# Whole rows of the last expert weights, two engines in source order, and copies out of two PSUM banks in a chunked-attention, MoE and soft-MoE kernel

## Chip, cores, metric

One core of one Trainium2 chip. The metric is device time in microseconds (us) of one launch, median over runs. Engines: TensorE (PE), VectorE (DVE), ScalarE (ACT), GpSimd (POOL), SyncE (SP, which here only issues DMAs).

## What is computed

Three layers in a row, all in float32 at the interface:

```python
out  = softmax(scale * q_c @ k_c.T) @ v_c          # chunks of 64 in a sequence of 576, 8 batches, 8 heads
x    = square(relu(x @ w_in)) @ w_out              # 4608 x 512, inner width 2048
logits = x @ phi                                   # 4608 x 32 (8 experts, 4 slots each)
d    = softmax over the 4608 tokens;  slot_input = d.T @ x          # 32 x 512
h_e  = relu(slot_input_e @ w1[e]);  slot_out_e = h_e @ w2[e]        # w1: 8 x 512 x 1024, w2: 8 x 1024 x 512
out  = softmax over the 32 slots (logits) @ slot_out                # 4608 x 512
```

The expert weights w1 and w2 are 16.78 MB each, the output is 9.44 MB.

## The kernel before

36 token tiles of 128 tokens (two batches of 64 tokens each) go through attention and the first MoE layer in blocks of three, a long pipeline that ends when the last block's logits are there. The change lies behind that point, in three stages.

**The chain.** `soft(b)` (lines 849 to 952) takes a block's logits, scales them (`Ls`, L854), spreads them by a matmul (L864), takes the largest (L874 to L876), forms `dts` by an exponential (L877), turns it (L917), and adds `dd` times the tiles `G` to the running sum `acc` (24 records of L928, then L939). For the last block, `slot_turn` (L803) transposes `acc` into one PSUM bank, `slot_rows_of` (L811) multiplies by w_out (`wo`) into another, `slot_inputs` (L824) makes `siT`. Both copies out of PSUM go through `halves` (L799): ScalarE takes the left half of the bank, VectorE the right. Beside the chain, `c_two` prepares four of nine groups of transposed token weights `cT`: a PE transpose (L1047), two ScalarE copies each (L1055, L1060), a subtraction on POOL (L1061) and POOL copies (L197) for the next two groups.

**The experts.** 32 units of w1 and 32 of w2, 512 KB each, are loaded by SP in the order of `units`, each into two free half buffers of 128 x 512 floats. A unit goes as one DMA if the two halves lie side by side (L985 for w1, L994 for w2), else as two (L988, L999). Buffers come free by `give` and `release`: the last four `G` tiles, which hold six units, once L928 has read them, the `wo` buffers once `slot_rows_of` has, and then each weight after its matmul. A unit of w2 is a column half: 4 x 128 rows by 256 columns, so each piece is 1 KB. All of column half 0 is multiplied first (L1584 into `sop`), then all of half 1.

**The output.** Once a column half is summed, `slot_rows` and `slot_parts` form `s4_h[ch]` (ScalarE L1492, PE L1497, ScalarE L1499, VectorE L1501), and `out_group` multiplies it by `cT` (L1553), copies to `o` (L1555 VectorE, L1557 ScalarE) and stores 128 x 4 x 256 pieces (L1568). The four tiles that straddle batches ("lone") go as eight DMAs of 64 KB per column half (L1574).

**Order.** In the tail PE runs in source order by hand (`ST_ORDER`). ScalarE, VectorE, POOL and SP run in the order that a scheduler with a timeline model of its own chose when the program was built.

Of the kernel before, what the change touches and what calls it, by code (L numbers as in the profile page):

```python
# [20 lines left out]
P = 128  # L21
CH = 64
# [52 lines left out]
def kernel(  # L75
# [723 lines left out]
    def halves(out, in_):  # L799
        n = in_.shape[-1] // 2  # L800
        act.activation(out=out[:, :n], in_=in_[:, :n], func=ACTF.Copy)
        dve.tensor_copy(out[:, n:], in_[:, n:])

    def slot_turn():
        ps = misc()
        for c in range(QF):
            pe.transpose(ps[:, c * P : (c + 1) * P], acc[:, c * P : (c + 1) * P], ident)
        fin["yz"] = yz = big.tile([P, 2, DM], F32, tag="g1", name="yz")
        yT = yz[:, 0]
        halves(yT, ps)  # L810

    def slot_rows_of():
        ps = misc()
        yT = fin["yz"][:, 0].rearrange("p (c g s) -> p c g s", c=QF, s=NS)
        for c in range(QF):
            for g in range(NQ):
                pe.matmul(
                    ps[NS * g : NS * g + NS], yT[:, c, g], wo[QF * g + c],
                    start=(c == 0), stop=(c == QF - 1), tile_position=(0, NS * g),
                    skip_group_check=True,  # L820
                )
        halves(fin["yz"][:, 1], ps)
# [26 lines left out]
    def soft(b):  # L849
        s0, n = blocks[NB if b == 1 else b]  # L850
        last = s0 + n == NT
        L, iv = L_ps.pop(b), iv2_all[:, s0 : s0 + n]
# [105 lines left out]
    RT = 1024 // DH  # L958
    units = [(0, 0, 4 * g + e, kk) for g in range(2) for kk in range(KT) for e in range(4)]
# [10 lines left out]
    def load_units():  # L970
        while todo and len(free) > 1:

            whole = [x for x in range(len(free) - 1) if free[x][0] is free[x + 1][0]]
            x = whole[0] if whole else 0
            a, b = free[x : x + 2]
            del free[x : x + 2]
            u = todo.pop(0)
            m, ch, e, kk = u
            whole_home = a[0] is b[0] and a[1] + 512 == b[1]
            places = [t[:, o : o + 512] for t, o, _ in (a, b)]  # L980
            home[u] = (a, b)
            if m == 0:
                src = w1[e, kk * P : (kk + 1) * P, :]
                if whole_home:
                    sp.dma_start(out=a[0][:, a[1] : a[1] + 1024], in_=src)  # L985
                else:
                    for h, pl in enumerate(places):
                        sp.dma_start(out=pl, in_=src[:, h * 512 : (h + 1) * 512])  # L988
            else:
                src = w2[e, kk * RT * P : (kk + 1) * RT * P, ch * DH : (ch + 1) * DH].rearrange(  # L990
                    "(t p) d -> p t d", p=P
                )
                if whole_home:
                    sp.dma_start(  # L994
                        out=a[0][:, a[1] : a[1] + 1024].rearrange("p (t d) -> p t d", d=DH), in_=src
                    )
                else:
                    for h, pl in enumerate(places):
                        sp.dma_start(  # L999
                            out=pl.rearrange("p (t d) -> p t d", d=DH), in_=src[:, h * RT // 2 : (h + 1) * RT // 2]  # L1000
                        )
# [443 lines left out]
    def hidden_T(g, hs):  # L1445
        hT_g[g] = take([P, FT, P], F32, "hT")
        for h in range(2):
            htp = ps2.tile([P, FT // 2, P], F32, tag=f"ht{h}", name="htp")
            for ft in range(FT // 2):
                f0 = (h * FT // 2 + ft) * P  # L1450
                pe.transpose(htp[:, ft], hs[:, f0 : f0 + P], ident)
# [10 lines left out]
    for g in range(2):  # L1462
        hps_g[g] = [ps2.tile([P, 512], F32, tag=f"eh{g}{h}", name="ehps") for h in range(2)]
        for kk in range(KT):
            for hf in range(2):
                for ei in range(4):
# [3 lines left out]
                        part_of((0, 0, e, kk), hf),  # L1470
# [3 lines left out]
                for ei in range(4):  # L1474
                    release((0, 0, 4 * g + ei, kk), hf)
# [32 lines left out]
    GT = 1536 // DH  # L1508
    out_groups, lone = [], []
    for bp in range(NT // CPB):  # L1510
        i0 = bp * CPB
        pairs = [i for i in range(i0, i0 + CPB) if i % 2 == 0 and in_pairs(i)]
        lone += [(i, None) for i in range(i0, i0 + CPB) if not in_pairs(i)]
        for c in range(2):
            group_ = [(i, c) for i in pairs]
            if not out_groups:

                out_groups.append(group_[:2])
                group_ = group_[2:]
            out_groups.append(group_)  # L1520
        if len(lone) == 4:
            out_groups.append(lone)
            lone = []
    assert not lone

    def out_buffer():

        if not todo:
            tags = [t for _, _, t in free]
            for tag in tags:  # L1530
                if size_of[tag] == 1024 and tags.count(tag) == 2:
                    free[:] = [x for x in free if x[2] != tag]
                    return big.tile([P, 4, DH], F32, tag=tag, name="o")
        group_no[0] += 1
        return big.tile([P, GT, DH], F32, tag=out_tags[group_no[0] % 3], name="o")

    step = 512 // DH
    BANKS = sum(-(-len(x) // step) for x in out_groups)
    banks = ("eh00", "eh01", "eh10", "eh11", "ht0")
    bank, group_no = [0], [0]  # L1540

    def out_group(ch, x):

        parts = out_groups[x]
        n = len(parts)
        o = out_buffer()
        for j0 in range(0, n, step):
            m = min(step, n - j0)
            ops = ps2.tile([P, step, DH], F32, tag=banks[bank[0] % 5], name="ops")
            for j in range(m):  # L1550
                i, c = parts[j0 + j]
                rows = cT[i // 8][:, i % 8 + (c or 0)]
                pe.matmul(ops[:, j], rows, s4_h[ch], start=True, stop=True)  # L1553
            if bank[0] % 2:
                dve.tensor_copy(o[:, j0 : j0 + m], ops[:, :m])  # L1555
            else:
                act.activation(out=o[:, j0 : j0 + m], in_=ops[:, :m], func=ACTF.Copy)  # L1557
            bank[0] += 1
            yield

        def at_(i, c):
            bp, ci = divmod(i, CPB)
            return (2 * bp + c) * S + ci * CH

        cols = slice(ch * DH, (ch + 1) * DH)
        if parts[0][1] is not None:
            r0 = at_(*parts[0])
            sp.dma_start(  # L1568
                out=out[r0 : r0 + n * P, cols].rearrange("(t p) d -> p t d", p=P), in_=o[:, :n]
            )  # L1570
        else:
            for j, c in ((j, c) for j in range(n) for c in range(2)):
                r0 = at_(parts[j][0], c)
                sp.dma_start(out=out[r0 : r0 + CH, cols], in_=o[CH * c : CH * c + CH, j])  # L1574

    pending, outs = None, []
    for ch in range(NCH):
        sop = ps2.tile([P, DH], F32, tag=f"so{ch % 2}", name="sop")
        for x in range(2 * FT):
            g, ft = divmod(x, FT)  # L1580
            kk, t = divmod(ft, RT)
            for ei in range(4):
                u = (1, ch, 4 * g + ei, kk)
                pe.matmul(  # L1584
                    sop[32 * ei : 32 * ei + 32], hT_g[g][:, ft, 32 * ei : 32 * ei + 32],
                    part_of(u, t // (RT // 2))[:, t % (RT // 2) * DH : (t % (RT // 2) + 1) * DH],
                    start=(x == 0), stop=(x == 2 * FT - 1),
                    tile_position=(0, 32 * ei), skip_group_check=True,
                )
            if (t + 1) % (RT // 2) == 0:  # L1590
                for ei in range(4):
                    release((1, ch, 4 * g + ei, kk), t // (RT // 2))
                load_units()
            if waiting and x == 1:
                hidden_T(*waiting.pop())
            if pending and x == 0:
                slot_parts(*pending)
                outs = [out_group(ch - 1, y) for y in range(len(out_groups))]
                pending = None
                n_out = 0  # L1600

            if outs and c_todo and x > 1 and x % 2:
                c_group(c_bank("ht1"))
            while outs and n_out < (x - 2) * BANKS // (2 * FT - 3):
                n_out += 1
                while outs and next(outs[0], StopIteration) is StopIteration:
                    outs.pop(0)
        pending = (ch, slot_rows(ch, sop))
        while outs:
            while outs and next(outs[0], StopIteration) is StopIteration:  # L1610
                outs.pop(0)
    slot_parts(*pending)
    for y in range(len(out_groups)):
        for _ in out_group(NCH - 1, y):
            pass
# [30 lines left out]
```

## Time and profile before

| | us |
|---|---|
| median of 3 runs | 772.77 (772.29 to 775.29) |
| profiled execution, its own time | 774.87 |
| profiled execution, span | 773.1 |
| PE busy | 711.1 (92%) |
| DMA queue of SP, time of its packets | 57.7% of 16 engines' span |

PE is busy for 92% of the span, but that is an average over stages. The page's 40 slices of 19.3 us each tell the stages apart: in the last four the DMA engines are full and PE is not.

### The profile page before, as it was taken

What the parts mean: (1) busy time and instruction counts of PE and PEld (TensorE: products, weight loads), DVE (VectorE), ACT (ScalarE), POOL (GpSimd) and SP (SyncE); (2) the same over time, 40 slices, a digit from 0 to 9 for tenths busy, and PEclk for the clock granted to TensorE, in tenths of its full rate; (3) what the DMA queues carried; (4) which work ended last, traced back from release to release, by engine and by line L of the source; (5) the groups of instructions that cost most, each with busy time, mean ns of one, the idle gap of its engine ahead of it and who ended that gap; (6) DMA issues with size and microseconds to landing.
All of it is one profiled execution on the core that took longest, in us unless ns stands there. A gap on an engine that the chain in (4) does not pass through costs nothing.

```text
span 773.1 us, 16704 instructions
## 1 busy us (share of the span) xinstructions
PE 711.1 (92%) x6612; PEld 457.7 (59%) x6612; DVE 428.1 (55%) x908; ACT 457.3 (59%) x951; POOL 161.9 (21%) x209
## 2 busy tenths in 40 slices
PE   5788999898999999999999999999999999969790
PEld 3677776665666566565665656666666565524350
DVE  4789996267756656567665566566656201012160
ACT  3668787664656666666676566566766555531150
POOL 3222221131222312223132231322223100030000
PEclk9799999999999999999999999999999999999995
DMA  7897933233455534455544655454556523759998
GB/s 158 215 257 180 218 123 124 72 66 83 98 117 103 103 76 97 91 103 104 101 97 83 103 101 112 75 103 89 99 88 171 159 69 112 277 178 354 347 355 255
DMA packets 242589, 110.47 MB, mean 143 GB/s; under 512 B 201808, under 2 KB 235600, under 8 KB 242512
## 3 DMA queue, kind: packets, MB, share of 16 engines
q1 hardware_dynamic: 242512, 109.41, 57.7%
q8 instruction: 52, 0.85, 0.5%
q14 instruction: 25, 0.20, 0.1%
HBM read 78.71 MB, written 9.44 MB: 114 GB/s over the span
## 4 chain that ended last, share of the span: by engine, by line
PE 71%; DMA 10%; DVE 9%; ACT 4%; issue 1%; POOL 1%; SPq 1%; DVEq 0%; POOLq 0%; ACTq 0%
PE hps L727 41%; PE gT L761 7%; PE misc L928 4%; PE L L778 4%; DMA unit<-in_moe_w_dram 3%; PE ehps L1468 2%; DVE qk L276 2%; DMA qkT<-qk 2%; DMA qkv<-in_k_dram 2%; DMA qkv<-in_q_dram 1%; PE misc L332 1%; DMA qkv<-in_v_dram 1%; DVE stage L281 1%; PE misc L498 1%; DVE qk L275 1%
## 5 line engine op out<-in xcount | busy, mean ns | idle before, releaser
L727 PE MATMUL hps<-xb,wi 128*128 128x384 f16 (+2 forms) x2400 | 409.2, 321 | 0.3
L727 PEld LDWEIGHTS <-wi 128*128 128x128 f16 x2400 | 225.1, 98 | 139.9 <-issue 18.3
L742 ACT ACTIVATE g<-hps,inv_w 128x384 f32<-128x384 f32 (+1 forms) x200 | 112.6, 563 | 113.0 <-PE hps L727 110.8
L182 DVE TENSOR_REDUCE am<-qkv 128x1 bf16<-128x512 f32 x90 | 61.9, 687 | 89.9 <-DMA qkv<-in_v_dram 45.8
L188 ACT ACTIVATE G<-gT 128x384 f32<-128x384 f32 (+1 forms) x200 | 94.1, 471 | 17.9 <-PE gT L761 15.3
L761 PE MATMUL gT<-ident,g 128*128 128x128 f32 x576 | 98.3, 278 | 4.6 <-ACT G L188 3.7
L749 ACT ACTIVATE g<-g 128x384 f32<-128x384 f32 (+2 forms) x188 | 96.9, 515 | 1.5
L761 PEld LDWEIGHTS gT<-ident,g 128*128 128x128 f32 x576 | 73.0, 144 | 29.6 <-ACT g L749 7.1
L420 POOL TENSOR_SCALAR vbd<-qkv,as 64x512 f16<-64x512 f32 x54 | 37.2, 689 | 87.5 <-PE misc L500 71.8
L471 POOL TENSOR_TENSOR ex<-ex,rs 128x512 f32<-128x512 f32 x27 | 29.3, 1083 | 122.4 <-DVE rs L468 110.3
L410 DVE SCALAR_TENSOR_TENSOR qk<-qkv,as,qk 128x512 f16<-128x512 f32 x54 | 39.7, 762 | 20.4 <-ACT qk L405 19.8
L425 DVE SCALAR_TENSOR_TENSOR vbd<-qkv,as,vbd 64x512 f16<-64x512 f32 x54 | 44.7, 828 | 0.7
L778 PE MATMUL L<-g,wp 128*32 128x384 f32 x384 | 41.7, 498 | 0.0
L405 ACT ACTIVATE qk<-qkv,as 128x512 f16<-128x512 f32 x54 | 36.8, 717 | 7.9 <-DVE as L215 7.9
L484 POOL TENSOR_TENSOR p<-ex,p 128x512 f16<-128x512 f32 x27 | 36.2, 1341 | 16.5 <-ACT p L481 15.9
L481 ACT ACTIVATE p<-ex 128x512 f16<-128x512 f32 x27 | 17.0, 629 | 34.6 <-POOL ex L471 34.4
L928 PE MATMUL misc<-G,dd 128*32 128x512 f32 x288 | 35.1, 622 | 0.5 <-DVE rs__8963 L936 0.5
L435 DVE COPY qbd<-qkT 64x1024 f16<-64x1024 f16 x54 | 23.3, 431 | 18.3 <-DMA qkT<-qk 17.5
L510 DVE SCALAR_TENSOR_TENSOR xb<-misc,xb 128x512 f16<-128x512 f32 x27 | 18.5, 685 | 26.5 <-ACT xb L504 26.2
L223 POOL TENSOR_SCALAR iv_all<-ai 128x1 f32<-128x1 f32 x27 | 7.4, 273 | 108.5 <-DVE ai L218 107.6
L854 DVE TENSOR_TENSOR Ls<-L,iv_all 128x384 f32<-128x384 f32 x12 | 6.7, 557 | 41.5 <-PE L L778 41.5
L461 ACT ACTIVATE ex<-ex,es 128x512 f32<-128x512 f32 x27 | 19.4, 718 | 17.0 <-DVE ex L455 16.9
(156 smaller groups left out, 1018.9 us busy)
## 6 DMA issues: line engine op xcount, KB each, us to landing
unit<-in_moe_w_dram SPq DMA_DIRECT2D x34, 512.0 KB, 4.5
unit<-in_moe_w_dram SPq DMA_DIRECT2D x60, 256.0 KB, 5.9
qkv<-in_q_dram SPq DMA_DIRECT2D x72, 128.0 KB, 3.3
qkv<-in_k_dram SPq DMA_DIRECT2D x72, 128.0 KB, 3.5
qkv<-in_v_dram SPq DMA_DIRECT2D x72, 128.0 KB, 3.3
stage<-in_moe_w_in_dram SPq DMA_DIRECT2D x16, 512.0 KB, 5.3
stage<-in_moe_w_out_dram SPq DMA_DIRECT2D x16, 512.0 KB, 5.8
out_dram<-o SPq DMA_DIRECT2D x14, 512.0 KB, 6.3
```

The source lines that it names most:

```text
L182: dve.tensor_reduce(out=am, in_=src, axis=AX.X, op=ALU.max, apply_absolute_value=True)
L188: act.activation(out=out, in_=in_, func=ACTF.Copy)
L405: act.activation(out=qk16[:, 2 * a], in_=flat[:, a], func=ACTF.Copy, scale=v["s"][:, a : a + 1])
L410: dve.scalar_tensor_tensor(out=qk16[:, 2 * a + 1], in0=flat[:, a], scalar=v["s"][:, a : a + 1], in1=qk16[:, 2 * a], op0=ALU.mult, op1=ALU. ...
L420: pool.tensor_scalar(out=dst[0], in0=vin, scalar1=v["s"][pr, 2:3], scalar2=1.0, op0=ALU.mult, op1=ALU.mult,)
L425: dve.scalar_tensor_tensor(out=dst[1], in0=vin, scalar=v["s"][pr, 2:3], in1=dst[0], op0=ALU.mult, op1=ALU.subtract,)
L727: pe.matmul(hp, wi[f][:, wl, kt], xb[:, xl, kt], start=(nm == 0), stop=(nm == 3 * KT - 1))
L742: act.activation(out=g, in_=hp, func=ACTF.Relu, scale=sc)
L749: act.activation(out=g, in_=g, func=ACTF.Square)
L761: pe.transpose(gt_ps[b, f][:, j], g[:, j * P : (j + 1) * P], ident)
L778: pe.matmul(L_ps[g0][NS * x : NS * x + NS, :n], wp[:, QF * q + x], g[:, x, :n], start=(q == 0), stop=(q == NQ - 1), tile_position=(0, NS * x),
L928: pe.matmul(y[NS * g : NS * g + NS], dd[:, j], G_q[b, g][:, j], start=(j == 0), stop=(j == n - 1), tile_position=(0, NS * g), skip_group_c ...
```

## The change

1. From the last `soft` on, ScalarE and VectorE also run in source order (`tc.manual_schedule`).
2. `halves` becomes `half_out`: the left and right halves of `acc` transposed, and of the product with `wo`, go into two PSUM banks. ScalarE copies the first bank while PE fills the second, which VectorE copies. The product is 32 matmuls of 256 columns instead of 16 of 512.
3. The units of w2 are whole rows (256 rows x 512 columns, partition p holding rows 2p and 2p+1, 4 KB that lie together) for all of expert group 0 and the first quarter of group 1: 20 units. The last 12 are column halves again, each for four experts. Both column sums are kept at once.
4. The output is stored in another order: column half 0 of batches 0 to 3 while the last weights of half 1 arrive, then whole rows of the lone tiles and of batches 4 to 7, then column half 1 of batches 0 to 3. The five late `cT` groups are made while w2's rows arrive.

```diff
-    def halves(out, in_):
-        n = in_.shape[-1] // 2
-        act.activation(out=out[:, :n], in_=in_[:, :n], func=ACTF.Copy)
-        dve.tensor_copy(out[:, n:], in_[:, n:])
+    def half_out(h, out, in_):
+        copy(("act", "dve")[h], out[:, h * DM // 2 : (h + 1) * DM // 2], in_)
...
+        for h in range(2):
+            ps = misc()[:, : DM // 2]
+            for x in range(QF // 2):
+                c = h * QF // 2 + x
+                pe.transpose(ps[:, x * P : (x + 1) * P], acc[:, c * P : (c + 1) * P], ident)
+            half_out(h, yz[:, 0], ps)
...
         last = s0 + n == NT
+        if last:
+            ctx.enter_context(
+                tc.manual_schedule(engines={mybir.EngineType.Activation, mybir.EngineType.DVE})
+            )
...
+    SPLIT = FT // 4
+    units = [("w1", 4 * g + e, kk) for g in range(2) for kk in range(KT) for e in range(4)]
     units += [
-        (1, ch, 4 * g + e, kk)
-        for ch in range(NCH) for g in range(2) for kk in range(FT // RT) for e in range(4)
+        ("rows", 4 * g + e, m)
+        for g in range(2) for m in range((SPLIT if g else FT) // 2) for e in range(4)
     ]
+    units += [("part", ch, ft) for ch in range(NCH) for ft in range(SPLIT, FT)]
+    def w2_rows(e, m):
+        return w2[e, 2 * P * m : 2 * P * (m + 1)].rearrange("(p t) d -> p t d", t=2)
...
+                src = w2[4:, 2 * P * m : 2 * P * (m + 1), ch * DH : (ch + 1) * DH].rearrange(
+                    "e (p t) d -> p t e d", t=2
+                )[:, ft % 2]
...
+    for ft in range(SPLIT, FT):
+        last_rows(0, ft)
+    slot_parts(0, slot_rows(0, sops[0]))
+    firsts = [quads[0][:2], quads[0][2:], *quads[1:]]
+    for ft in range(SPLIT, FT):
+        if FT - ft < len(firsts):
+            out_group(firsts.pop(0), (0,))
+        last_rows(1, ft)
+    so_sb = slot_rows(1, sops[1])
+    out_group(firsts.pop(0), (0,))
+    slot_parts(1, so_sb)
+    for rows in pairs:
+        out_group(rows, both)
+    for rows in quads:
+        out_group(rows, (1,))
```

ScalarE at the last soft-max, before (`cT` and `c` are the copies beside the chain, `dts` and `al` the exponentials, `yz` the chain's copies):

```order
L188 ACTIVATE G<-gT 128x3x128 x2
L1055 ACTIVATE cT<-cps 128x512
L1060 ACTIVATE c_8518<-cps 64x512
L1055 ACTIVATE cT<-cps 128x512
L1060 ACTIVATE c_8543<-cps 64x512
L877 ACTIVATE dts,rsum<-misc,nm 128x384
L880 ACTIVATE al<-run_m,nm 128x1
L1055 ACTIVATE cT<-cps 128x512
L1060 ACTIVATE c_8946<-cps 64x512
L1055 ACTIVATE cT<-cps 128x512
L1060 ACTIVATE c_8951<-cps 64x512
L801 ACTIVATE yz<-misc 128x256 x2
```

Here four copies beside the chain stand ahead of `dts`, and four ahead of `yz`. The same place in the change:

```order
L188 ACTIVATE G<-gT 128x3x128 x2
L882 ACTIVATE dts,rsum<-misc,nm 128x384
L885 ACTIVATE al<-run_m,nm 128x1
L1063 ACTIVATE cT<-cps 128x512
L1068 ACTIVATE c_8518<-cps 64x512
L1063 ACTIVATE cT<-cps 128x512
L1068 ACTIVATE c_8543<-cps 64x512
L188 ACTIVATE yz<-misc 128x256 x2
L1063 ACTIVATE cT<-cps 128x512
L1068 ACTIVATE c_8948<-cps 64x512
L1063 ACTIVATE cT<-cps 128x512
L1068 ACTIVATE c_8953<-cps 64x512
```

The exponentials move ahead of the first four copies, and the chain's two copies ahead of the second four. POOL's and PE's orders stay the same here, except that PE has 32 narrower matmuls for 16.

SP's last DMAs before, from the last of w1 on:

```order
L985 DMA unit<-in_moe_w_dram 128x1024 x5
L988 DMA unit<-in_moe_w_dram 128x512
L999 DMA unit<-in_moe_w_dram 128x2x256 x3
L994 DMA unit<-in_moe_w_dram 128x4x256 x8
L999 DMA unit<-in_moe_w_dram 128x2x256 x45
L1568 DMA out_dram<-o 128x2x256 x2
L1568 DMA out_dram<-o 128x4x256 x7
L1574 DMA out_dram<-o 64x256 x8
```

After these rows the last three come once more, for column half 1. In the change:

```order
L1004 DMA unit<-in_moe_w_dram 128x1024 x5
L1008 DMA unit<-in_moe_w_dram 128x512 x4
L1004 DMA unit<-in_moe_w_dram 128x1024 x8
L1008 DMA unit<-in_moe_w_dram 128x512 x21
L1008 DMA unit<-in_moe_w_dram 128x2x256 x22
L1004 DMA unit<-in_moe_w_dram 128x4x256
L1555 DMA out_dram<-o 128x2x256 x2
L1555 DMA out_dram<-o 128x4x256 x3
L1555 DMA out_dram<-o 128x2x512
L1563 DMA out_dram<-o 64x2x512 x4
L1555 DMA out_dram<-o 128x2x512 x7
L1555 DMA out_dram<-o 128x4x256 x4
```

The loads of rows have the shapes of w1's loads, and only the last 23 load DMAs have pieces of 1 KB. Of the stores, 16 of 64 KB become four of 256 KB.

## Rows read from the trace of the kernel before

**Rows 1.** The page: DMA busy tenths and GB/s in 40 slices.
```profile
DMA  7897933233455534455544655454556523759998
GB/s 158 215 257 180 218 123 124 72 66 83 98 117 103 103 76 97 91 103 104 101 97 83 103 101 112 75 103 89 99 88 171 159 69 112 277 178 354 347 355 255
```
**Rows 2.** Windows: start:end, length, busy per engine, PE clock, DMA share, GB/s.
```profile
657.00:661.00 4.00, 4.00 (x32) 2.39 (x25) 0.00 (x0) 2.09 (x5) 0.00 (x0) 1.00 1.01 393
677.00:686.00 9.00, 5.71 (x36) 2.06 (x35) 1.96 (x7) 3.07 (x8) 3.68 (x4) 0.81 0.01 4
683.00:684.00 1.00, 1.00 (x8) 0.22 (x4) 0.00 (x0) 0.00 (x0) 0.00 (x0) 0.50 0.00 0
692.00:694.00 2.00, 1.42 (x12) 0.98 (x8) 0.42 (x1) 0.38 (x1) 0.00 (x0) 1.00 0.93 286
696.00:712.00 16.00, 16.00 (x153) 6.17 (x146) 3.44 (x9) 2.12 (x5) 0.00 (x0) 1.00 1.10 356
712.00:740.00 28.00, 22.84 (x243) 11.48 (x242) 6.53 (x10) 6.37 (x12) 2.47 (x4) 1.00 1.09 347
745.00:751.00 6.00, 5.01 (x40) 3.78 (x36) 3.74 (x8) 3.55 (x8) 0.00 (x0) 1.00 1.09 385
752.00:756.00 4.00, 1.66 (x12) 1.33 (x11) 2.66 (x5) 2.06 (x4) 0.00 (x0) 1.00 0.62 187
756.00:768.00 12.00, 0.00 (x0) 0.00 (x0) 0.00 (x0) 0.00 (x0) 0.00 (x0) 0.53 1.03 337
768.00:772.00 4.00, 0.00 (x0) 0.00 (x0) 0.00 (x0) 0.00 (x0) 0.00 (x0) 0.50 0.53 126
```
**Rows 3.** Timeline of the last soft-max: start, us, engine, line, instruction [idle before].
```profile
676.61 0.60 ACT L1055 ACTIVATE cT<-cps 128x512 fp32r<-128x512 f32 x1 [2.32 <-PE cps L1047]
676.96 0.15 DVE L876 TENSOR_SCALAR nm<-rm 128x1 f32<-128x1 f32 x1
677.95 2.48 POOL L1061 TENSOR_TENSOR cT<-c,cT 64x512 fp32r<-64x512 f32 x2 [49.65 <-ACT c L1060]
679.07 0.58 ACT L877 ACTIVATE dts<-misc,nm 128x384 f32<-128x384 f32 x1
680.52 1.20 POOL L197 TENSOR_SCALAR c<-cmat 128x512 f32<-128x512 f32 x2
680.67 4.48 PE L928 MATMUL misc<-G,dd 128*32 128x512 f32 x24 [0.50 <-DVE rs__8963 L936]
685.08 1.09 PE L1047 MATMUL cps<-ident,c 128*128 128x128 f32 x8
```
**Rows 4.** Timeline of an earlier block: the same matmuls.
```profile
605.13 2.78 PE L928 MATMUL misc<-G,dd 128*32 128x512 f32 x24
```
**Rows 5.** Timeline, behind the sum: the chain's copies.
```profile
688.25 0.38 ACT L801 ACTIVATE yz<-misc 128x256 f32<-128x256 f32 x1
688.66 0.42 DVE L802 COPY yz<-misc 128x256 f32<-128x256 f32 x1 [2.62 <-ACT yz L801]
692.47 0.38 ACT L801 ACTIVATE yz<-misc 128x256 f32<-128x256 f32 x1 [3.84 <-PE misc L817]
```
**Rows 6.** Waits of SP's own queue: total us, times, longest.
```profile
SPq L985 <- PE misc L928: 16.8, 2, 12.1
```
**Rows 7.** Timeline of SP: issues of DMAs.
```profile
655.29 0.95 SPq L988 DMA_DIRECT2D unit<-in_moe_w_dram  x2
747.34 6.97 SPq L1574 DMA_DIRECT2D out_dram<-o  x8
763.61 7.11 SPq L1574 DMA_DIRECT2D out_dram<-o  x8
```
**Rows 8.** Timeline, from the last weights' matmuls to the first copies of outputs.
```profile
745.50 0.64 PE L1584 MATMUL sop<-unit,hT 128*32 128x256 f32 x8
749.19 5.47 DVE L1555 COPY o<-ops 128x512 f32<-128x512 f32 x9 [0.83 <-DMA out_dram<-o]
```

More of the change, by code (lines that the diff above doesn't have):

```diff
@@ L797, in prepare_final @@
             dve.memset(second[r : r + 32], -1.0)
-    def halves(out, in_):
-        n = in_.shape[-1] // 2
-        act.activation(out=out[:, :n], in_=in_[:, :n], func=ACTF.Copy)
-        dve.tensor_copy(out[:, n:], in_[:, n:])
+    def half_out(h, out, in_):
+        copy(("act", "dve")[h], out[:, h * DM // 2 : (h + 1) * DM // 2], in_)
     def slot_turn():
-        ps = misc()
-        for c in range(QF):
-            pe.transpose(ps[:, c * P : (c + 1) * P], acc[:, c * P : (c + 1) * P], ident)
         fin["yz"] = yz = big.tile([P, 2, DM], F32, tag="g1", name="yz")
-        yT = yz[:, 0]
-        halves(yT, ps)
+        for h in range(2):
[4 more added lines that the diff above has]
+            half_out(h, yz[:, 0], ps)
     def slot_rows_of():
-        ps = misc()
         yT = fin["yz"][:, 0].rearrange("p (c g s) -> p c g s", c=QF, s=NS)
[L815 to L822, printed above, removed]
+        for h in range(2):
+            ps = misc()[:, : DM // 2]
+            for c in range(QF):
+                for g in range(NQ):
+                    pe.matmul(
+                        ps[NS * g : NS * g + NS], yT[:, c, g],
+                        wo[QF * g + c][:, h * DM // 2 : (h + 1) * DM // 2],
+                        start=(c == 0), stop=(c == QF - 1), tile_position=(0, NS * g),
+                        skip_group_check=True,
+                    )
+            half_out(h, fin["yz"][:, 1], ps)
     def slot_inputs():
@@ L977, in load_units @@
             u = todo.pop(0)
-            m, ch, e, kk = u
             whole_home = a[0] is b[0] and a[1] + 512 == b[1]
-            places = [t[:, o : o + 512] for t, o, _ in (a, b)]
             home[u] = (a, b)
[L982 to L988, printed above, removed]
-            else:
[L990 to L1001, printed above, removed]
+            if u[0] == "w1":
+                _, e, kk = u
+                src = w1[e, kk * P : (kk + 1) * P, :].rearrange("p (h d) -> p h d", h=2)
+            elif u[0] == "rows":
+                src = w2_rows(*u[1:])
+            else:
+                _, ch, ft = u
+                m = ft // 2
+                src = w2[4:, 2 * P * m : 2 * P * (m + 1), ch * DH : (ch + 1) * DH].rearrange(
+                    "e (p t) d -> p t e d", t=2
+                )[:, ft % 2]
+            n = src.shape[1] // 2
+            if whole_home:
+                to = a[0][:, a[1] : a[1] + 1024].rearrange("p (t d) -> p t d", t=2 * n)
+                sp.dma_start(out=to, in_=src)
+            else:
+                for h, (t, o, _) in enumerate((a, b)):
+                    to = t[:, o : o + 512].rearrange("p (t d) -> p t d", t=n)
+                    sp.dma_start(out=to, in_=src[:, h * n : (h + 1) * n])
     def freed(pool_, tag, n):
@@ L1449, in hidden_T @@
             for ft in range(FT // 2):
-                f0 = (h * FT // 2 + ft) * P
-                pe.transpose(htp[:, ft], hs[:, f0 : f0 + P], ident)
+                m, t = divmod(h * FT // 2 + ft, 2)
+                rows = hs[:, 2 * P * m : 2 * P * (m + 1)].rearrange("p (x t) -> p t x", t=2)
+                pe.transpose(htp[:, ft], rows[:, t], ident)
             dst = hT_g[g][:, h * FT // 2 : (h + 1) * FT // 2]
@@ L1504, in slot_parts @@
         s4_h[ch] = s4
[L1508 to L1523, printed above, removed]
@@ L1524 @@
-    assert not lone
-    def out_buffer():
[L1528 to L1538, printed above, removed]
@@ L1539 @@
-    banks = ("eh00", "eh01", "eh10", "eh11", "ht0")
[L1540 to L1551, printed above, removed]
+    def out_buffer():
+        tags = [t for _, _, t in free]
+        for tag in tags:
+            if not todo and 512 * tags.count(tag) == size_of[tag] >= 1024:
+                free[:] = [x for x in free if x[2] != tag]
+                break
+        else:
+            tag = out_ring.pop(0)
+        out_ring.append(tag)
+        return big.tile([P, 1024], F32, tag=tag, name="o")
@@ new lines, with out_group @@
+    out_ring = list(out_tags)
+    banks = ("eh00", "eh01", "eh10", "eh11", "ht0")
+    bank = [0]
+    by_batch = out.rearrange("(b s) d -> s b d", s=S)
+    def out_group(parts, chs):
+        n, w = len(parts), len(chs) * DH
+        flat = out_buffer()
+        items = [(i, c, ch) for i, c in parts for ch in chs]
+        for x0 in range(0, len(items), 2):
+            ops = ps2.tile([P, 2, DH], F32, tag=banks[bank[0] % 5], name="ops")
+            for x, (i, c, ch) in enumerate(items[x0 : x0 + 2]):
@@ L1552, in out_group @@
                 rows = cT[i // 8][:, i % 8 + (c or 0)]
-                pe.matmul(ops[:, j], rows, s4_h[ch], start=True, stop=True)
+                pe.matmul(ops[:, x], rows, s4_h[ch], start=True, stop=True)
+            dst = flat[:, x0 * DH : (x0 + 2) * DH].rearrange("p (x d) -> p x d", x=2)
             if bank[0] % 2:
-                dve.tensor_copy(o[:, j0 : j0 + m], ops[:, :m])
+                dve.tensor_copy(dst, ops)
             else:
-                act.activation(out=o[:, j0 : j0 + m], in_=ops[:, :m], func=ACTF.Copy)
+                act.activation(out=dst, in_=ops, func=ACTF.Copy)
@@ L1558, in out_group @@
             bank[0] += 1
[L1559 to L1565, printed above, removed]
+        o = flat[:, : n * w].rearrange("p (t d) -> p t d", t=n)
+        cols = slice(chs[0] * DH, chs[0] * DH + w)
+        bp, ci = divmod(parts[0][0], CPB)
         if parts[0][1] is not None:
-            r0 = at_(*parts[0])
+            r0 = (2 * bp + parts[0][1]) * S + ci * CH
             sp.dma_start(
-                out=out[r0 : r0 + n * P, cols].rearrange("(t p) d -> p t d", p=P), in_=o[:, :n]
+                out=out[r0 : r0 + n * P, cols].rearrange("(t p) d -> p t d", p=P), in_=o
@@ L1570, in out_group @@
             )
         else:
[L1572 to L1588, printed above, removed]
+            s0, (bq, cj) = ci * CH, divmod(parts[-1][0], CPB)
@@ new lines, in out_group @@
+            assert n == 2 and ci == cj
+            for c in range(2):
+                to = by_batch[s0 : s0 + CH, 2 * bp + c : 2 * bq + c + 1 : 2 * (bq - bp), cols]
+                sp.dma_start(out=to, in_=o[CH * c : CH * c + CH])
+    both = tuple(range(NCH))
+    quads, pairs, lone = [], [], []
+    for bp in range(NT // CPB):
+        tiles_of = range(bp * CPB, (bp + 1) * CPB)
+        even = [i for i in tiles_of if i % 2 == 0 and in_pairs(i)]
+        lone += [(i, None) for i in tiles_of if not in_pairs(i)]
+        for c in range(2):
+            rows = [(i, c) for i in even]
+            if bp < 2:
+                quads.append(rows)
+            else:
+                pairs += [rows[x : x + 2] for x in range(0, len(rows), 2)]
@@ new lines, with rows_times @@
+    lone.sort(key=lambda x: x[0] % CPB)
+    pairs[1:1] = [lone[x : x + 2] for x in range(0, len(lone), 2)]
+    sops = [ps2.tile([P, DH], F32, tag=f"so{ch}", name="sop") for ch in range(NCH)]
+    def rows_times(g, ft, ch, rows):
+        for ei in range(4):
+            pe.matmul(
+                sops[ch][32 * ei : 32 * ei + 32], hT_g[g][:, ft, 32 * ei : 32 * ei + 32], rows(ei),
+                start=(g == 0 and ft == 0), stop=(g == 1 and ft == FT - 1),
+                tile_position=(0, 32 * ei), skip_group_check=True,
+            )
@@ L1589 @@
+    for g in range(2):
+        for ft in range(SPLIT if g else FT):
+            m, t = divmod(ft, 2)
+            for ch in range(NCH):
+                rows_times(
+                    g, ft, ch,
+                    lambda ei: part_of(("rows", 4 * g + ei, m), t)[:, ch * DH : (ch + 1) * DH],
                 )
-            if (t + 1) % (RT // 2) == 0:
+            if t:
                 for ei in range(4):
-                    release((1, ch, 4 * g + ei, kk), t // (RT // 2))
+                    release(("rows", 4 * g + ei, m), 0)
+                    release(("rows", 4 * g + ei, m), 1)
@@ L1593 @@
                 load_units()
-            if waiting and x == 1:
+            if waiting and ft == 1:
                 hidden_T(*waiting.pop())
[L1596 to L1602, printed above, removed]
-                c_group(c_bank("ht1"))
[L1604 to L1615, printed above, removed]
+            if c_todo and t:
+                c_group(c_bank("ht1"))
+    def last_rows(ch, ft):
+        u = ("part", ch, ft)
+        rows_times(1, ft, ch, lambda ei: part_of(u, ei // 2)[:, ei % 2 * DH : (ei % 2 + 1) * DH])
+        release(u, 0)
+        release(u, 1)
```

8 lines of the change are left out of this document (4 added, 4 removed).

## The prediction

> **What bounds the kernel now.** I read the page's slices first [rows 1]. Up to slice 34 the DMA engines are half busy and PE nearly full; from slice 36 on DMA stands at 9 tenths, and PE is no longer the limit. The windows by stage say where that begins and how fast it runs [rows 2]. From 677 to 686 the DMA engines move nothing (share 0.01), though SP has loads of weights to issue: its queue waits for L928, up to 12.1 us at a time [rows 6], since the `G` tiles that L928 reads are the next free buffers. Behind that the engines are full until 752: w2's column halves arrive at 347 GB/s (712 to 740), and the first stores leave at 385 (745 to 751). From 752 to 756 they fall to 187, because SP spends 6.97 us on issuing eight stores of 64 KB [rows 7]; from 756 to 768 the second half's stores run at 337, and from 768 to 772 the last eight small ones again starve the engines (126). So the tail is one long transfer that starts when the last sum over `G` ends. Two things set the time: when it starts, and how many microseconds its bytes take, holes included.
>
> Counted back from 772.0, the 9.44 MB of output fill 4 us at 126 GB/s (0.50 MB), 12 at 337 (4.04), 4 at 187 (0.75), and 4.15 MB at 385 (10.8 us): the stores begin at 741.2 and take 30.8 us [rows 2].
>
> About 0.5% (3.9 us) is what a measurement of this kernel can tell from no change. My sum is made in differences against the profiled execution (its own time 774.87, span 773.1). That execution is 2.1 us above the median of the three runs; I subtract the difference from the median, 772.77.
>
> **The change part by part.**
>
> *ScalarE's order.* Before, `nm` is ready at 676.96 + 0.15 = 677.11, but the exponential starts at 679.07, behind four copies for `cT` [rows 3]. In source order it goes first: 1.94 us earlier, and with it the sum L928, which started at 680.67 and then starts near 678.7.
>
> *The clock in that sum.* L928 took 4.48 us for 24 records [rows 3]; in an earlier block the same took 2.78 [rows 4]. The granted clock was 0.50 while it ran (683 to 684), the lower of the two levels, 1.2 GHz, after PE had done almost nothing from 677 to 680.7 [rows 2, 3]. In the change that pause is 1.94 us shorter and has a transpose in its middle. Gain between 0 and 4.48 - 2.78 = 1.70; I take 1.70, as the pauses of the pipeline, which stays at full clock, are nearer to what is left. L928 then ends at about 681.5 instead of 685.2, and SP's blocked loads start 3.64 us earlier.
>
> *A new wait, on POOL.* The copies that were moved back start behind `al`, near 678.0, and take 1.2 us for a pair; POOL follows with 2.48 and 1.20 us [rows 3], done near 683.0. PE's next instructions in its own order are the L1047 transposes of POOL's result, and `acc`'s turn is queued behind them. So PE stands from 681.5 to 683.0, and the chain wins 2.5 us, not 3.6. For DMA this costs nothing: the loads into `G` need only L928. Its six units (3.1 MB, 8 us at 385) last until about 690.5. By then `wo` must be free. Before, the two copies were done at 689.08 and the product lasted until 692.47 [rows 5], 3.8 us from its first input. In the change 24 of 32 matmuls must pass before the first `wo` pair is free, some 3 us, from about 684.5: 687.5; were each half as long as a whole product (7.6 us in all), 690.2. Covered.
>
> *Two banks.* VectorE's copy started only when ScalarE's had ended (688.66 behind 688.25 + 0.38 [rows 5]). The two-bank form hides one copy of 0.4 us at either place. It shortens the chain to `siT` but not the DMA's start, so I count it as nothing; cover is the queue of loads. Only the dip of 692 to 694 (286 instead of 356 GB/s [rows 2], 0.14 MB) should go, as `wo` comes in time: 0.4 us.
>
> *Whole rows of w2.* 20 of 32 units, 10.49 MB, go from 1 KB pieces to 4 KB (whole homes) or 2 KB (split). At 347 GB/s they take 30.2 us. The nearest rows are w1's loads of the same shapes: 393 GB/s from 657 to 661, among them split ones issued at 655.3 [rows 2, 7]. At 393 they take 26.7 us. Bounds: gain 0 (rate unchanged) to 3.5 us; I take 385, 27.25 us, a gain of 2.95. The Trainium skill (DMA: Bandwidth & Descriptors, section Specifications) speaks against this term: by its table transfers reach line rate from 512 B on, so 1 KB pieces would have nothing to gain and the term would be 0. The trace disagrees, with 347 against 393 GB/s at 1 KB and at 2 to 4 KB.
>
> *The last 12 units.* Same bytes and 1 KB pieces as before: 6.29 MB at 347, 18.1 us, no change. The matmuls are as many as before and have slack.
>
> *The output.* Column half 0 of batches 0 to 3 (2.10 MB) at 385: 5.45 us. Whole rows of the rest (5.24 MB): no row shows stores of 2 KB pieces; between the 337 of the slower 1 KB stores and the 393 of long loads, 15.5 to 13.3 us; I take 365, the middle: 14.4. Column half 1 of batches 0 to 3 (2.10 MB) at 337, as the second halves ran: 6.2. The 16 small stores become four, so the 187 and 126 GB/s stretches go; for the running out at the end I leave 0.5 us. One hole is new: whole rows need both column sums, so they wait behind the last weight. That path took 745.50 to 749.9 (749.19 and one copy of 0.69 from VectorE's nine in 5.47, with its gaps) [rows 8], 4.4 us, plus four matmuls of the last half-0 group on PE and a DMA's start, some 6 us by estimate. Queued to cover it are the 5.45 us of half-0 stores, of which the last 0.5 MB is issued late. Hole between 0 and 5 us; I take 1.5, since four of the five groups are issued before the last weight lands. Sum 5.45 + 14.4 + 6.2 + 0.5 + 1.5 = 28.05 us against 30.8: 2.75 less.
>
> *Source order on VectorE, and the five late `cT` groups among the rows.* VectorE's order at the chain does not change. The late groups are 1.2 us each on ScalarE and VectorE together, beside loads of 5 us a step: nothing.
>
> **Sum.** 1.94 + 1.70 + 0.4 + 2.95 + 2.75 = 9.7 us: 772.77 - 9.7 = **763.1 us**.
>
> **The rivals.**
> 1. *Piece length does not matter.* The rows load at 347, and the whole-row stores leave at 337. For it: the row with 356 from 696 to 712 has a share of 1.10, more than 393 had (1.01), so the engines are busy per byte in a way that may not be the pieces'. Against: w1's loads. 2.95 + 1.1 lost: 767.2 us. The Trainium skill's rule above would give this case.
> 2. *The hole stays uncovered*, 5 us instead of 1.5: SP issues the half-0 stores in order behind the loads, and PE multiplies them between rows that wait for DMA. Against: four groups are due before the last weight. 766.6 us.
> 3. *The transfer does not start earlier*: the order moves, but the sum or its buffers come as late as before, through the slow clock and another wait. For it: the low clock was there before. Against: nothing but `nm` holds the exponential. 3.64 lost: 766.7 us.
> 4. *The last 12 units become slow*, the one on the other side. Each now gathers four experts' 1 KB pieces, 2 MiB apart. The worst full stretch of loads in the trace is the start (218 GB/s at 9 tenths, short pieces [rows 1]): 6.29 MB take 28.9 us instead of 18.1, and the time is 773.9, slower than before. It decides from 226 GB/s down (18.1 + 9.7 us). Against: the column units before were 1 KB pieces too, with gaps. The Trainium skill (DMA: Bandwidth & Descriptors, section Latency and other measured facts) reports 164 GB/s where partitions lie 2 MiB apart, which by estimate would make 38 us of this and 783 in all; here it is the experts that lie so, partitions are 4 KB apart, and no row shows either.
>
> **How the numbers follow.** Forecast with its bounds (clock, rates, hole) 66%; rival 1 13%, rival 2 9%, rival 3 7%, rival 4 5%. The forecast's own bounds: all rates at 385 to 393 and no hole give 759.5, low clock and stores at 337 give 766. The range 760.0 to 768.5 takes in the first three rivals and leaves out the fourth, pairs of rivals, and the best corner: some 15%. Faster by over 0.5% means below 768.9: the forecast and nearly all of rivals 1 to 3, 86%. Within 0.5%: pairs of them and half of rival 4, 10%. Slower: the rest of rival 4, 4%.
>
> **What would show it.** Right: the exponential within 0.1 us of `nm`; L928's 24 records in 2.8 us at clock 1.00; PE standing some 1.5 us ahead of L1055's transposes; DMA share near 0 for about 5 us, not 9; 380 GB/s or more while rows arrive, 350 in the last 12 units; no stretch at 126 at the end. Wrong: rows at 350 (rival 1), several microseconds of share under 0.5 after the last weight (rival 2), a DMA start near 686 (rival 3), or under 230 GB/s in the last units (rival 4).

## The result and the profile after

The changed kernel takes 762.82 us (median of 4 runs, 761.28 to 764.96) against 772.53 (4 runs, 772.03 to 775.29): ratio 0.9872, 95% interval 0.9842 to 0.9901. A second set of six runs on another occasion gave 764.59 against 772.42, ratio 0.9901 (0.9874 to 0.9928). So the change takes 1.0 to 1.3% off; the forecast was 763.1.

The total mixes two things. The stretch up to the last logits holds the same instructions in the same order on every engine, yet the profiled executions reach `Ls` of the last block at different times: 674.61 us before, 672.91 after, and between 671.1 and 674.1 in the kernels tried below, whose instructions up to there are the same as well. Below I therefore compare **tails**, from the start of that `Ls` to the end of the span: 98.5 us before, 90.3 after, 8.2 less.

The timeline of the changed kernel at the last soft-max (start, us, engine, line, instruction, idle time before):

```profile
672.91 0.56 DVE L859 TENSOR_TENSOR Ls<-L,iv_all 128x384 f32<-128x384 f32 x1 [19.86 <-PE L L778]
675.25 0.15 DVE L881 TENSOR_SCALAR nm<-rm 128x1 f32<-128x1 f32 x1
675.44 0.58 ACT L882 ACTIVATE dts<-misc,nm 128x384 f32<-128x384 f32 x1 [2.86 <-DVE nm L881]
676.89 2.78 PE L933 MATMUL misc<-G,dd 128*32 128x512 f32 x24 [0.35 <-DVE rs__8965 L941]
680.13 1.20 POOL L197 TENSOR_SCALAR c<-cmat 128x512 f32<-128x512 f32 x2
680.80 1.24 PE L1055 MATMUL cps<-ident,c 128*128 128x128 f32 x8 [1.14 <-POOL c L197]
682.36 0.38 ACT L188 ACTIVATE yz<-misc 128x256 f32<-128x256 f32 x1 [3.73 <-PE misc L808]
682.52 0.42 DVE L193 COPY yz<-misc 128x256 f32<-128x256 f32 x1 [1.96 <-PE misc L808]
687.82 0.29 DVE L832 COPY siT<-misc 128x128 f32<-128x128 f32 x1 [0.79 <-PE misc L828]
```

They answer to [rows 3, 5]. The exponential follows `nm` at once, where it stood behind four copies. The sum over `G` takes 2.78 us instead of 4.48. PE then waits 1.14 us for POOL's copies, the new wait that was foretold. VectorE's copy no longer waits for ScalarE's.

The windows of the changed kernel (start:end, length, busy per engine, PE clock, DMA share, GB/s), against [rows 2]:

```profile
676.00:680.00 4.00, 3.15 (x27) 0.93 (x27) 1.13 (x6) 2.56 (x7) 2.48 (x2) 1.00 0.01 4
690.00:702.00 12.00, 12.00 (x110) 4.62 (x106) 2.75 (x8) 1.48 (x3) 0.22 (x1) 1.00 1.03 409
704.00:712.00 8.00, 7.12 (x100) 4.27 (x96) 2.16 (x4) 2.08 (x4) 1.22 (x2) 1.00 1.01 347
718.00:733.00 15.00, 13.33 (x98) 4.49 (x94) 1.86 (x3) 1.96 (x4) 0.00 (x0) 1.00 1.08 347
734.00:736.00 2.00, 1.85 (x17) 1.14 (x17) 0.69 (x1) 1.05 (x3) 0.00 (x0) 1.00 0.72 249
738.00:740.00 2.00, 2.00 (x17) 1.90 (x16) 1.67 (x3) 1.91 (x4) 0.00 (x0) 1.00 0.82 280
742.00:746.00 4.00, 3.79 (x26) 3.21 (x24) 4.00 (x8) 3.99 (x8) 0.00 (x0) 1.00 0.94 267
748.00:754.00 6.00, 0.00 (x0) 0.00 (x0) 0.00 (x0) 0.00 (x0) 0.00 (x0) 0.68 1.04 391
756.00:761.00 5.00, 0.00 (x0) 0.00 (x0) 0.00 (x0) 0.00 (x0) 0.00 (x0) 0.50 1.02 342
```

The idle stretch of the DMA engines, nine microseconds before, is about four and a half (share 0.01 from 676 to 680; the first bytes come at 680.5), and TensorE's clock stays at 1.00. Rows in whole homes (their two half buffers lie side by side, so that a piece is 4 KB) arrive at 409 GB/s, the last column halves at 347. Two dips behind the last weight, at 734 and 738, are the hole: stores wait there for the second column sum. Then come three kinds of stores: the lone tiles at 267, whole rows at 391, column half 1 at 342. The stretch at 126 GB/s at the end is gone. SP's wait for the sum fell from 12.1 us at the longest [rows 6] to 8.4. Its wait for the product that frees the `wo` buffers did not fall:

```profile
SPq L1004 <- PE misc L933: 8.4, 1, 8.4
SPq L1004 <- PE misc L817: 2.0, 1, 2.0
```

Before, that second wait was 1.8 us. The loads still dip shortly behind it, to between 287 and 307 GB/s from 687.0 to 688.5.

### The profile page after: what moved, and what is told of

The parts are those of the page before. It is cut to its first block, busy times and chain, and to the rows that moved or that the text cites. A ratio compares the mean times of both kernels' runs of the same rounds, so it can differ in the third digit from the quotient of the medians.

```text
span 763.2 us, 16746 instructions
## 1 busy us (share of the span) xinstructions
PE 707.3 (93%) x6644; PEld 457.2 (60%) x6644; DVE 426.7 (56%) x908; ACT 457.4 (60%) x951; POOL 162.6 (21%) x209
## 3 DMA queue, kind: packets, MB, share of 16 engines
HBM read 78.71 MB, written 9.44 MB: 115 GB/s over the span
## 4 chain that ended last, share of the span: by engine, by line
PE 68%; DMA 11%; DVE 10%; ACT 2%; POOL 2%; issue 2%; SPq 1%; DVEq 0%; POOLq 0%; ACTq 0%
PE hps L727 41%; PE gT L761 7%; PE L L778 4%; DMA unit<-in_moe_w_dram 4%; PE misc L933 4%; DMA qkv<-in_k_dram 2%; PE ehps L1477 2%; DVE qk L276 2%; DMA qkT<-qk 2%; DMA pT<-p 1%; DMA qkv<-in_v_dram 1%; PE misc L498 1%; DVE stage L281 1%; DVE o L1546 1%; DVE qk L275 1%
## 5 line engine op out<-in xcount | busy, mean ns | idle before, releaser
L188 ACT ACTIVATE G<-gT 128x384 f32<-128x384 f32 (+1 forms) x200 | 94.1, 471 | 17.6 <-PE gT L761 14.9
L749 ACT ACTIVATE g<-g 128x384 f32<-128x384 f32 (+2 forms) x188 | 96.8, 515 | 1.5
L471 POOL TENSOR_TENSOR ex<-ex,rs 128x512 f32<-128x512 f32 x27 | 29.2, 1083 | 123.5 <-DVE rs L468 111.1
L435 DVE COPY qbd<-qkT 64x1024 f16<-64x1024 f16 x54 | 23.6, 437 | 19.2 <-DMA qkT<-qk 18.7
L933 PE MATMUL misc<-G,dd 128*32 128x512 f32 x288 | 33.4, 596 | 0.4 <-DVE rs__8965 L941 0.4
```

Of the source, the lines that this page charges most:

```text
L188: act.activation(out=out, in_=in_, func=ACTF.Copy)
L749: act.activation(out=g, in_=g, func=ACTF.Square)
L933: pe.matmul(y[NS * g : NS * g + NS], dd[:, j], G_q[b, g][:, j], start=(j == 0), stop=(j == n - 1), tile_position=(0, NS * g), skip_group_c ...
```

## The experiments

The theory: three separate gains, an earlier start of one long transfer (order and clock), faster loads (piece length), faster stores. Its rivals: piece length does not matter; the earlier start is given back; the hole or the last units eat the gain. The table is worked out from each kernel's trace in windows of half a microsecond: "start" is from the last `Ls` to the first bytes behind the idle stretch; counted back from the last byte, 9.44 MB are the outputs, and what lies between start and there are the loads (19.2 MB in every kernel). The windows make each of the three good to about half a microsecond. The medians come from four occasions, on which the kernel before stood between 771.81 and 772.76 us.

| kernel | tail | start | loads | outputs | median of runs |
|---|---|---|---|---|---|
| before | 98.5 | 11.4 | 55.1 | 30.9 | 772.53 |
| order_only | 94.8 | 7.8 | 54.9 | 31.1 | 769.88 |
| before_warm | 96.8 | 9.5 | 55.1 | 30.9 | 772.79 |
| no_order | 93.7 | 11.1 | 52.2 | 28.8 | 768.67 |
| the change | 90.3 | 7.6 | 52.5 | 29.0 | 762.82 |
| after_again (the change) | 90.3 | 7.5 | 52.3 | 29.2 | 764.59 |
| one_bank | 88.9 | 7.4 | 51.8 | 28.2 | 764.52 |
| rows_1k | 93.3 | 7.3 | 55.7 | 28.8 | 766.44 |
| lone_as_pairs | 88.5 | 7.5 | 52.3 | 27.2 | 763.40 |
| whole_release | 89.0 | 7.6 | 51.7 | 28.8 | 762.83 |
| whole_early_s4 | 88.8 | 7.6 | 51.6 | 28.4 | 762.81 |
| whole_early | 88.9 | 7.4 | 51.6 | 28.9 | 762.93 |
| whole_early_lone | 88.9 | 7.4 | 51.3 | 28.7 | 763.00 |

What remains of each tail, some 0.9 to 1.6 us, lies behind the last byte. In windows of 0.1 us it is 1.1 to 1.3 us in every kernel, and the outputs take 30.7 us before, 29.0 and 29.3 in the change's two profiles, 28.5 in one_bank, 27.5 in lone_as_pairs and 29.0 in whole_early_lone.

### The order alone, and the change without it

order_only, on the kernel before:

```diff
         last = s0 + n == NT
+        if last:
+            ctx.enter_context(
+                tc.manual_schedule(engines={mybir.EngineType.Activation, mybir.EngineType.DVE})
+            )
```

> The kernel before, with ScalarE and VectorE in source order from the last soft-max on and nothing else. If the order alone starts the transfer earlier, by 2 us through the exponential and 1.7 through the clock of the sum over G, the tail from the last logits to the end is 98.5 - 3.8 = 94.7 us and the time about 768.8; the loads' and stores' rates stay at 347 and 337 to 385 GB/s. If the order was worth nothing and rows and stores made the whole gain, the time stays at 772.5.

The tail is 94.8 us, 3.7 less than before, and all of it lies in the start (7.8 for 11.4): loads and outputs take what they took. The runs' ratio is 0.9953 (0.9934 to 0.9973), 769.88 us.

no_order takes the same lines out of the changed kernel.

> The changed kernel without the source order on ScalarE and VectorE: the four copies for cT stand ahead of the exponential again. If order and bytes are two separate gains, the sum over G ends 10.7 us after the last logits instead of 6.9, at a clock of 0.50, and the tail grows from 90.3 to about 94 us, the time to about 766.6. If the earlier start is given back further on (by wo, or by the chain), the time stays at 762.8.

The tail is 93.7, 3.4 more than with the order, again in the start alone. Its median is 768.67 us, 2 us above the 766.6 expected. From before to no_order the tail falls 4.8 us, from before to order_only 3.7; together 8.5, and the whole change gives 8.2. The gains are separate and add up.

### The clock of the sum over G

before_warm, on the kernel before:

```diff
         if last:
             c_two(0)
+            warm = ps_t.tile([P, 512], F32, tag="gT", name="warm")
+            for x in range(16):
+                pe.transpose(warm[:, x % 4 * P : (x % 4 + 1) * P], ident, ident)
```

> The kernel before with 16 extra transposes of the identity in TensorE's pause ahead of the sum over G, into a bank that nobody reads; the exponential stays behind the copies. If the pause is what lowered the clock, the 24 records of the sum take 2.8 us instead of 4.5 at a clock of 1.00, the transfer starts 1.7 us earlier, and the time is about 770.8. If the clock falls for another reason, the sum takes 4.5 us again and the time is 772.5 or more.

The timeline of before_warm:

```profile
676.23 1.91 PE L890 MATMUL warm<-ident 128*128 128x128 f32 x16
678.46 0.58 ACT L877 ACTIVATE dts<-misc,nm 128x384 f32<-128x384 f32 x1
680.06 2.78 PE L931 MATMUL misc<-G,dd 128*32 128x512 f32 x24 [0.52 <-DVE rs__8980 L939]
```

The sum starts as late as before, 6.07 us behind `Ls` (before: 6.06), yet takes 2.78 us at a granted clock of 1.00 instead of 4.48 us, most of them at 0.50. The pause lowered the clock, and 1.70 us is its price. In no_order, with the pause and without the transposes, the sum took 4.34 us and the clock fell to 0.50 again. The tail of before_warm is 1.7 us shorter, as expected. The median of its runs is not (772.79 against 772.76, ratio 0.9982 to 1.0024): the expected 0.9978 lies just outside. So the trace shows the gain and the medians do not; why stays open.

### One PSUM bank

one_bank puts `halves`, `slot_turn` and `slot_rows_of` of the kernel before into the changed kernel.

> The changed kernel with the chain's copies out of one PSUM bank again and 16 matmuls of 512 columns. The forecast priced the two banks at nothing: siT comes about 0.8 us later, the wo buffers are free at about the same time, the transfer starts as before and the time stays within 1 us of 762.8. If the chain to siT sets the transfer, the time grows by what siT loses, to about 763.6 to 764.5.

`siT` comes 15.5 us after `Ls` instead of 14.9, so the two banks shorten the chain by 0.6 us, and the transfer does not care: it starts within 0.2 us of the same point, and its median (764.52) lies between the change's two (762.82 and 764.59). Its tail is even 1.4 us shorter, in loads and outputs. The change's own two profiles agree on a tail of 90.3, so this may be more than the difference between two executions. SP's wait for the product is 1.5 us with one bank and 2.0 with two. The forecast's price of nothing is within what the runs resolve; whether the second bank costs a part of that 1.4 us is not settled.

### The length of the pieces

rows_1k loads the same rows, in the same order, into the same places, in two column halves each:

```diff
-                src = w2_rows(*u[1:])
+                src = w2_rows(*u[1:]).rearrange("p t (h d) -> p h t d", h=2)
...
-            if whole_home:
+            if u[0] == "rows":
+                for h, (t, o, _) in enumerate((a, b)):
+                    to = t[:, o : o + 512].rearrange("p (t d) -> p t d", t=2)
+                    sp.dma_start(out=to, in_=src[:, h])
+            elif whole_home:
...
```

> The changed kernel with w2's whole-row units loaded as two column halves each, 40 DMAs of 256 KB with pieces of 1 KB, into the same buffers and in the same order of units and outputs. If the length of the pieces makes the rows' rate, the 10.49 MB go at 348 GB/s instead of about 385, the tail from the last logits to the end grows by about 2.9 us over the changed kernel's (90.3 and, with one bank, 88.9), and the time is about 765.7. If piece length does not matter (rival 1), the tail stays at 89 to 91 us.

Windows of rows_1k, the rows and then the last units among them:

```profile
692.00:704.00 12.00, 12.00 (x116) 4.29 (x117) 2.93 (x9) 2.07 (x4) 0.00 (x0) 1.00 1.09 356
706.00:734.00 28.00, 22.97 (x231) 9.59 (x230) 4.65 (x7) 4.95 (x9) 1.86 (x3) 1.00 1.09 347
```

The rate is the old one, the loads take 55.7 us as before the change, and the tail is 3.0 us longer: 766.44 us, against 762.81 to 763.40 for the three other kernels of the same occasion. Rival 1 falls; the pieces make the rate. The size of a DMA does not, at this length: with 1 KB pieces, DMAs of 512 KB ran at 354 GB/s in the kernel before (695 to 703), and those of 256 KB at 353 here (693 to 701).

whole_release lets both halves of a w1 step go together, so that the rows find whole homes:

```diff
-                for ei in range(4):
-                    release(("w1", 4 * g + ei, kk), hf)
-                load_units()
+            for ei in range(4):
+                for hf in range(2):
+                    release(("w1", 4 * g + ei, kk), hf)
+            load_units()
```

> The changed kernel with the buffers of w1 released after both halves of a step instead of after each, so that nearly all units of w2 find two halves side by side and rows come in pieces of 4 KB instead of 2 KB. If 4 KB pieces go faster than 2 KB ones (about 415 against 385 GB/s), 5.5 MB take 1.1 us less and the tail is about 1 us shorter; if pieces of 2 KB and more are alike, it stays at 89 to 91 us. The later release should cost nothing, since the queue of loads is full then.

Its windows, and the same stretch of after_again, where the homes are split:

```profile
704.00:712.00 8.00, 7.12 (x100) 4.09 (x96) 2.08 (x3) 1.97 (x4) 0.69 (x2) 1.00 1.03 408
```

```profile
704.00:712.00 8.00, 7.12 (x108) 4.36 (x100) 2.54 (x4) 1.79 (x3) 1.24 (x2) 1.00 1.05 385
```

4 KB pieces go at 408, 2 KB at 385, 1 KB at 347. (The split ones are also DMAs of 256 KB instead of 512; no run separates the two at 2 and 4 KB.) The loads are 0.6 us shorter than after_again's and the tail 1.3; 762.83 us stands beside 764.59 and 762.82 of the change's sets on other occasions, with intervals that overlap (0.9853 to 0.99 against 0.9874 to 0.9928 and 0.9842 to 0.9901). A small gain, not settled by the runs.

after_again is the changed kernel a second time.

> The changed kernel once more, unchanged, beside the others. In its first profile the rows fell from 410 to 340 to 354 GB/s between 704 and 712, which no other kernel with the same loads shows. If that was that execution's own, the loads take 51.8 to 52.3 us here instead of 52.5, the tail is about 89 us and the median 762 to 764. If it belongs to the two banks or to the earlier siT, it comes back.

The fall to 347 between 704 and 712 in the change's first profile did not come back (385 above), so it was that execution's own. The loads take 52.3 us, but the tail is 90.3 again, because the outputs take 29.2: its hole is deeper, 234 GB/s from 732 to 736. The median, 764.59, is above the 762 to 764 expected.

### The stores

lone_as_pairs:

```diff
-        if parts[0][1] is not None:
-            r0 = (2 * bp + parts[0][1]) * S + ci * CH
+        if True:
+            r0 = (2 * bp + (parts[0][1] or 0)) * S + (ci if parts[0][1] is not None else 0) * CH
...
```

> The changed kernel with the two stores of lone tiles done as ordinary ones: 512 KB from 128 partitions to 256 rows in a row, instead of two of 256 KB from 64 partitions each. The rows of the lone tiles thus land in wrong places, and four tiles of the output stay unwritten: only the time is meant. If the dip to 263 to 271 GB/s while the lone stores leave comes from their half set of partitions, it goes, and the tail is 1.0 to 1.4 us shorter than the changed kernel's. If it comes from the mix of half rows and whole rows or from where they lie in memory, the dip stays.

Its window over the lone stores:

```profile
742.00:746.00 4.00, 4.00 (x28) 3.50 (x27) 4.00 (x8) 3.99 (x8) 0.00 (x0) 1.00 1.04 386
```

With 128 partitions the same 1 MB leaves at 386 GB/s, not 267, and the outputs take some 1.5 to 2.0 us less than the change's (27.2 us in the table, 27.5 in the finer windows). The tail is 1.8 us shorter, more than the 1.0 to 1.4 expected; the median, 763.40, does not show it. The dip belongs to these stores' form: half the partitions, 256 KB each, and each partition's two rows of 2 KB going to two batches. Which of these it is, this run does not separate.

whole_early_s4 adds to whole_release four more units as rows and earlier first stores:

```diff
-    SPLIT = FT // 4
+    SPLIT = FT // 2
...
-        if FT - ft < len(firsts):
+        for _ in range({FT - 4: 2, FT - 3: 2, FT - 2: 1}.get(ft, 0)):
             out_group(firsts.pop(0), (0,))
         last_rows(1, ft)
     so_sb = slot_rows(1, sops[1])
-    out_group(firsts.pop(0), (0,))
```

> The kernel of whole_release with two more edits: four more units of w2 as whole rows (8 column-half units are left, not 12), and the five groups of half-0 stores made two, two and one ahead of the last rows instead of one per step and one behind them. If the hole behind the last weight comes from stores that are issued too late, the dips to 249 and 280 GB/s at 734 to 736 and 738 to 740 shrink and give 0.5 to 1 us; the units give 2.1 MB x (1/347 - 1/410) = 0.9 us. Together with whole_release about 2.5 us under the changed kernel, about 760. If the shorter time between the two column sums leaves the first stores late, the hole grows and takes it back.

Loads and outputs are as in whole_release within 0.4 us; 762.81 us, not the 760 expected. Two holes now:

```profile
728.00:732.00 4.00, 3.62 (x35) 2.40 (x36) 2.31 (x4) 1.83 (x4) 0.00 (x0) 1.00 0.79 257
736.00:738.00 2.00, 2.00 (x17) 1.85 (x15) 2.00 (x4) 2.00 (x5) 0.00 (x0) 1.00 0.56 197
```

With 6 us between the column sums the first stores miss the last weight, and the old hole comes after them. whole_early keeps the 12 units and only stores earlier.

> The kernel of whole_release with the five groups of half-0 stores made two, two and one ahead of the last rows, and 12 column-half units as in the changed kernel. With 9 us between the two column sums the first stores should be queued when the last weight lands: the outputs take 28.2 us instead of 28.8, the loads 51.7, the tail 88.3 us, about 762. If the hole is the path behind the last weight itself (rows times s4, then copies, 5 us) that 2 MB of stores cannot cover, the outputs take 28.8 again.

Outputs 28.9, no gain (762.93 us): 2 MB of half-0 stores, issued this much earlier, still do not cover the path behind the last weight. whole_early_lone issues the lone stores from ScalarE (`act.dma_start` for `sp.dma_start`).

> The kernel of whole_early with the four lone stores issued from ScalarE's own DMA queue, so that they run beside SP's stores of whole rows rather than alone. The stores that went to 128 partitions made the outputs 27.2 us. If stores from 64 partitions are slow only while nothing else runs beside them, outputs take about 27 us here and the time is some 1.2 us under whole_early. If ScalarE's copies wait behind its DMA issues, the copies come late, the stores starve, and it is as slow or slower.

```profile
736.00:742.00 6.00, 3.10 (x17) 2.63 (x17) 2.87 (x5) 2.28 (x6) 0.00 (x0) 0.89 0.82 252
```

The stores starve while PE is busy for 3.10 of 6 us and ScalarE for 2.28: the outputs take 28.7 us, and the median is 763.00. Whether stores from 64 partitions are slow only when they run alone stays open.

No run takes back the new order and form of the stores alone. That their gain comes from the small stores that went is read from the windows (the stretches at 187 and 126 GB/s are gone) and not shown by an experiment. No version tried beats the changed kernel by more than the runs resolve.

## Why the prediction was right

By its own terms, from `Ls` on:

- *Exponential first*, 1.94 us: the sum starts 3.98 us behind `Ls` instead of 6.06, 2.08 less. Shown by order_only and no_order together with before_warm, which takes the clock's share apart.
- *Clock*, 1.70 of 0 to 1.70: 2.78 against 4.48 us, shown apart by before_warm.
- *POOL's new wait*, 1.5 us and costed at nothing: 1.14 us, and the transfer started by the sum's end, 3.8 us earlier (forecast 3.64).
- *Two banks*, nothing: one_bank's start and median agree; its shorter tail is not explained.
- *Whole rows*, 2.95: the loads are 2.7 us shorter in the change's first profile, 2.8 in its second, and 2.9 and 3.3 in two kernels with the same loads (no_order 52.2, one_bank 51.8). Counted back by bytes, the 10.49 MB of rows took 27.4 and 26.8 us in the change's two profiles, 383 and 392 GB/s, about the 385 assumed. It is made up of 409 for whole homes, 385 for split ones, and slower stretches. rows_1k gave it all back, 3.0 us of tail.
- *The dip*, 0.4: it did not go. The prediction had `wo` free in time ("covered"), but SP waits 2.0 us for the product in the change against 1.8 before, and the loads dip as they did. This term was not earned.
- *The last 12 units*, no change: 347 GB/s, as taken. Rival 4 did not come.
- *The output*, 2.75: 1.7 and 1.8 in the change's own two profiles, 2.2 to 2.7 in one_bank, by the width of the windows. This term was sized too large for the change, and its parts were off both ways. Whole rows left at 391, above the 365 taken. Half 0 was to leave at 385 and left at 344. The lone stores were not priced apart and ran at 267. The hole, 1.5 us, was about 0.9 us in one profile (0.19 MB and 0.13 MB missing at 345 GB/s) and 1.6 in the other.

The sum, 9.7 us, stands against 8.2 in the tails, and 9.7 and 7.8 in the two sets of medians. The mechanism was right and its terms, the dip apart, were there, but the sum was about 1.5 us too large. That the first median meets the forecast to 0.3 us is thus in part luck: the second set stands 1.5 us above it. In the two profiled executions the whole time differs by 9.9 us, of which 1.7 come from the front, where the instructions are the same.

Of the rivals, 1 was refuted by rows_1k, 3 by the start in every kernel with the order, 4 by the rate; 2 is true in kind and small in size (0.9 and 1.6 us of hole against 5).

## What to carry to other kernels

When a stage is one long transfer, ask first what lets it start, and which engine's queue delays that: here two exponentials behind four copies nobody waited for. A pause of TensorE can be paid twice, as the pause and as the slower clock of what follows: here an exponential 2 us earlier was worth 3.8 us, since the sum behind it also ran at a granted clock of 1.00 (2.4 GHz) instead of mostly 0.50 (1.2 GHz). Then price the bytes by the length of the contiguous pieces, from a stretch of the same trace that has the longer pieces.

## What was not expected

- In the change's two profiles stores of 256 KB from 64 partitions went at 263 to 273 GB/s, those of 512 KB from 128 partitions to whole rows at 386 to 391.
- Column-half stores of one shape, 128 x 4 x 256, ran at 385 GB/s in the kernel before (745 to 751) and at 344 in the change (736 to 739); no run explains it.
- Gathering four experts' 1 KB pieces that lie 2 MiB apart cost nothing: 347 GB/s, as for the old units.
- The part of the program that no edit touches ended up to 3.5 us apart from one profiled kernel to another (0.4 us between the change's own two profiles), more than several of the effects sought here. What moves it stays open.
